# Spreading the rows of a routing list over steps of attention and products of TensorE

## The chip, the cores and the metric

The kernel runs on one core of one Trainium2 chip. The metric is the device time of one execution in microseconds; several executions are made and their median is given. Beside them one execution is taken with the hardware profiler, which records every instruction of the core's engines and every DMA packet.

## The reference: linear attention, then a mixture of experts with sticky routing

Attention has 8 batches, 8 heads, 576 positions and 64 features a head. Queries and keys are projected to 128 features, less the largest magnitude of the row, and both signs are exponentiated, so 256 features come out. For each head `kv` is the sum over positions of features times values, `z` the sum of features, and the output is `q_phi @ kv / (q_phi @ z + 1e-6)`. The heads are laid side by side: 4608 tokens of 512 features.

Each token then goes to one of 8 experts. It takes the expert with the largest gate logit, or, where a second gate's sigmoid is at least 0.5, the expert of the token before it (within its batch). The expert is `relu(x @ w1[e]) @ w2[e]` with 1024 hidden features, and its output is scaled by the softmax weight of that expert's logit.

```python
e = fresh_e if s == 0 or local_gate[b, s] < 0.5 else prev_e
out[b, s] = p[e] * (np.maximum(x[b, s] @ w1[e], 0.0) @ w2[e])
```

## The kernel before, in words

**Attention.** Method `step` runs once for each pair of 128-position chunks, 72 steps in all, and writes TensorE's order out by hand: a projection (line 351), turning queries (371), sums of keys and values (403), and numerators (483) of earlier pairs. The logits of two batches are complete after every 18 steps and go to `gate(bp)`, bp 0 to 3.

**Gates.** `gate` is a generator: each `yield STEP` ends its share of one step, and `chores` (from `step`) advances each generator in the list `background` once a step. It finds each token's expert and its rank in the expert's list (four small TensorE products, lines 738, 750, 767, 780 to 785, each needing a small PSUM space of which there is one a step, `turn_comes`). At its end it writes the list: nine indirect DMAs from GpSimd's queue (line 836), each scattering 128 rows (token number, weight, 64 bytes a row) into the DRAM tensor `lst`. One transfer is issued a step. `paced` puts each behind a copy on GpSimd (`tick`, line 646) that waits for that step's maxima.

**Early plan.** `plan_early`, a fourth generator, waits until gate 1's rows are written (`while self.scattering`), holds two more steps, gathers six pieces of the list (line 902), waits three steps, turns them on TensorE (line 933), and gathers the tokens' rows (line 1223) one a step. They feed two early slots e0 and e1 of three times 128 tokens each. Meanwhile the weights of e0 are split into high and low parts (lines 575 and 577), half a tile a step.

**Tail.** After the last step `tail` is set. Gate 2's generator in `background` has rows left: after `drained` it issues at most five (`ROW`) at once and holds the others until gate 3's ranks are out. Gate 3 (`last_gate`) is advanced by hooks inside slot e0's first layer: `soon[0]` is a list of functions, and `layer1` calls one at each of its 16 pauses (two for each block f of hidden features). The eleventh, `rest`, runs gate 3 to its end, and gate 2's held rows between. All these rows go to GpSimd's queue one behind the other, with no other wait than gate 3's ranks.

**Main plan.** In e0's second layer `later[0]` begins with `listed`, which advances `plan_main` twice: the plan itself (a chain of small VectorE operations from line 996 on, after the product of line 942), then `fetch`: row numbers, the list gathers `lr<-lst` (line 902, each made to wait for every row scattered), and between them `duals`, the plan of half-filled pieces (lines 1066 to 1091). Then follow the three transposes (line 1252) of e1's tokens. `layer2` calls the next function behind the blocks f = 0 and f = 2 of each piece of 128 tokens. In e1's first layer `read`, at the tenth pause, turns the gathered list on TensorE (line 933), and the main slots' rows are gathered after it.

**Order of the rest.** From the tail on a scheduler orders each engine's instructions by when they are ready in its own forecast, within the edges that `issue_after` and `behind_it` set (the second is a semaphore wait). An engine runs its queue in that order.

Of the kernel before, what the change touches and what calls it, by code (L numbers as in the profile page):

```python
# [39 lines left out]
QUOTA = 16  # L40
LINE = 256

STEP = "step"

# [35 lines left out]
class Kernel:  # L82
# [9 lines left out]
    def run(self):  # L92
        nc, tc, A = self.nc, self.tc, self.A
        act, dve = self.act, self.dve
        with ExitStack() as root:
# [38 lines left out]
            n = NBP * NHP * NC  # L134
# [36 lines left out]
            plan = self.plan_main()  # L171
            go = self.advance

            def rest():
                for _ in self.last_gate:
                    if self.ranked is not None:
                        for x in self.background:
                            for _ in x:
                                pass

            def listed():
                next(plan)
                next(plan)

            def read():
# [2 lines left out]
            no = lambda: None  # L188
            m = []
# [13 lines left out]
            def singles():  # L203
                more()
                m[0]()
            self.slots(self.eslots, soon=[[no, no, no, go, no, no, go, no, no, go, rest],
                                          [no] * 9 + [read, a[0], a[1], no, a[2], no, a[3]]],
                       later=[[listed], [no, no, singles] + [lambda k=k: m[k]() for k in (1, 2, 3)] + [more]])
            back.close()
            self.mid.close()  # L210
            self.open_rest(root)
# [487 lines left out]
    def gate(self, bp):  # L699
# [123 lines left out]
        tc.keep_in_program_order(dve.tensor_copy(pr[:, :, 0], self.tokid[:, bp * NC:bp * NC + NC]))  # L823
        dve.tensor_mul(pr[:, :, 1], se, su)
        self.scattering = True
        for c in range(NC):
            yield STEP
            while self.tail and not self.drained:
                yield STEP
            if self.tail and self.ranked is None:  # L830
                self.late += 1
                while self.late > ROW and self.ranked is None:
                    self.held_back = True
                    yield STEP
            with self.paced():
                ins = pool.indirect_dma_start(self.lst[:, :], bass.IndirectOffsetOnAxis(ri[:, c:c + 1], 0),
                                              pr[:, c, :], None)
            if self.late > ROW:
                self.behind_it(ins, self.ranked, "it would hold the last gate's chain")
            tc.declare_no_dep(ins.ins, group="scatter", reason="scattered rows are distinct")  # L840
            tc.add_to_no_dep_group("scatter", ins.ins)
            self.scattered.append(ins)
# [543 lines left out]
    def layer2(self, s, between, held=None):  # L1386
        tc, dve, pool = self.tc, self.dve, self.pool
        hh, hl = s["h"]
        self.need(s, 8) if len(s["ei"]) == 1 else None
        for k in range(s["n"]):  # L1390
            if hasattr(self, "psr"):
                t = self.psr.tile([128, DM], F32, name="l2")
            else:
                t = self.psb.tile([128, DM], F32, name="l2", tag="nm")
            m = min(128, s.get("cols", s["n"] * 128) - k * 128)
            o = slice(k * 128, k * 128 + m)
            for f in range(8):
                c = slice((f % 2) * DM, (f % 2) * DM + DM)
                self.both(s, 4 + f // 2, t[0:m], hh[:, f, o], hl[:, f, o], c, f == 0, f == 7)
                if f in ((0, 2) if s["n"] > 1 else (1, 3, 5)) and between:  # L1400
                    between.pop(0)()
                if f % 2 and k == s["n"] - 1:
                    self.used(1)
                elif f % 2:
                    self.spare()
            last = held is not None and k == s["n"] - 1
            y = self.mx2.tile([128, DM], F32, name="yl", bufs=1) if last else self.mx2.tile([128, DM], F32, name="y")
            u = s["u"] + k
            if last:
                w = s["prob"][0:m, u:u + 1]  # L1410
                self.act.activation(y[0:m], t[0:m], AF.Copy, scale=w)
            elif hasattr(self, "psr"):
                self.marks[dve] = dve.tensor_scalar_mul(y[0:m], t[0:m], s["prob"][0:m, u:u + 1])  # L1413
            else:
                self.marks[self.act] = self.act.activation(y[0:m], t[0:m], AF.Copy, scale=s["prob"][0:m, u:u + 1])
                self.last_y = self.marks[self.act]

            def put(y=y[0:m], at=s["tok"][0:m, u:u + 1]):
                ins = pool.indirect_dma_start(self.A["out"], bass.IndirectOffsetOnAxis(at, 0), y, None,  # L1419
                                              bounds_check=NT - 1, oob_is_err=False)  # L1420
                tc.declare_no_dep(ins.ins, group="outs", reason="each token is written once")
                tc.add_to_no_dep_group("outs", ins.ins)
            if last:
                held.append(put)
            else:
                put()

    def slots(self, order, held=None, soon=(), later=()):
# [19 lines left out]
        for i, s in enumerate(order):  # L1448
# [16 lines left out]
            else:  # L1465
                self.layer1_two(s, [])
            if i < len(later):
                rest = list(later[i]) + rest
            self.layer2(s, rest, None if new else held)
            for f in rest:  # L1470
                f()
# [132 lines left out]
```

## Time and profile before

| | us |
|---|---|
| median of 3 runs | 715.51 |
| lowest, highest | 713.83, 719.53 |
| the profiled execution, its own time | 712.14 |
| its span, first to last instruction | 710.3 |
| TensorE busy, weight loads busy | 698.4, 617.9 |
| VectorE, ScalarE, GpSimd busy | 460.7, 411.8, 265.0 |

The profiled execution lies 3.37 us under the median; 1.84 us of its time lie outside the span. The views are a page of totals; tables of waits; tables of busy time by stretch; and the instructions in order of time. An instruction row gives its start and duration, the engine, the line, what it writes and reads, the shapes and the count; in brackets stands the idle time before it and what ended it.

### The profile page before, as it was taken

To read this page: it belongs to the slowest core of one execution; us is meant where nothing else is said; L and a number is where in the kernel's file an instruction comes from. 1 tells how busy PE (TensorE), PEld (TensorE's weight loads), DVE (VectorE), ACT (ScalarE), POOL (GpSimd) and SP (SyncE) were. 2 spreads that over 40 slices of the span, in tenths; PEclk is the share of its full clock that TensorE was granted. 3 is DMA by queue.
4 is the path that set the end of the run, shared out by engine and by line. 5 is a ranking of instruction groups with operands and counts; after the bars stand their busy time and mean duration, and the time that the engine had idled before them with its cause. 6 is when DMAs were issued, how large, how long until landed. Compare 5 with 4: busy or idle time off the path is not lost. (4 is left out here: it accounts for less than half of the span.)

```text
span 710.3 us, 22974 instructions
## 1 busy us (share of the span) xinstructions
PE 698.4 (98%) x9576; PEld 617.9 (87%) x9576; DVE 460.7 (65%) x876; ACT 411.8 (58%) x888; POOL 265.0 (37%) x532
## 2 busy tenths in 40 slices
PE   7999999999999999999999999999999999999996
PEld 6999999999999999888887986889888877888985
DVE  6898899889998995683537446535643367554522
ACT  5777776777768873434465654745754269471512
POOL 0211101430146675562345551345744236443311
PEclk9999999999999999999999999999999999999998
DMA  7855545555466863254818975344886375444200
GB/s 232 268 154 148 160 124 155 148 149 161 134 183 198 252 189 113 64 181 129 280 70 294 405 279 194 135 149 150 265 307 252 110 243 172 150 163 155 76 27 31
DMA packets 66074, 125.17 MB, mean 176 GB/s; under 512 B 7180, under 2 KB 45260, under 8 KB 65910
## 3 DMA queue, kind: packets, MB, share of 16 engines
q1 hardware_dynamic: 57680, 100.90, 44.8%
q0 software_dynamic: 7968, 22.58, 9.0%
q8 instruction: 76, 1.25, 0.7%
q14 instruction: 30, 0.25, 0.1%
q10 hardware_dynamic: 320, 0.20, 0.1%
HBM read 102.11 MB, written 21.80 MB: 174 GB/s over the span
## 5 line engine op out<-in xcount | busy, mean ns | idle before, releaser
L1173 DVE TENSOR_TENSOR wlo<-wraw,whi 128x1024 fp32r<-128x1024 f32 x80 | 96.4, 1222 | 37.8 <-ACT whi L1170 37.5
L1305 PE MATMUL l<-whi,hh 128*128 128x512 f32 (+1 forms) x288 | 113.4, 394 | 0.5 <-ACT hh L1358 0.5
L1306 PE MATMUL l<-wlo,hh 128*128 128x512 f32 (+1 forms) x288 | 112.7, 391 | 0.8 <-DVE wlo L1173 0.8
L1307 PE MATMUL l<-whi,hl 128*128 128x512 f32 (+1 forms) x288 | 112.6, 391 | 0.0
L362 ACT ACTIVATE kp<-sb 128x512 f32<-128x512 f32 x144 | 83.3, 623 | 48.9 <-DVE sb L359 48.1
L1359 DVE SCALAR_TENSOR_TENSOR hl<-l,hh 128x512 fp32r<-128x512 f32 (+3 forms) x84 | 50.4, 600 | 93.2 <-ACT hh L1358 93.1
L1170 ACT CAST whi<-wraw 128x1024 fp32r<-128x1024 f32 x80 | 82.4, 1047 | 43.8 <-PE l L1307 27.0
L1358 ACT ACTIVATE hh<-l 128x512 fp32r<-128x512 f32 (+3 forms) x84 | 44.0, 525 | 108.9 <-PE l L1307 57.2
L1305 PE MATMUL l<-xhi,whi 128*128 128x384 f32 (+4 forms) x308 | 106.8, 347 | 0.0
L1307 PE MATMUL l<-xhi,wlo 128*128 128x384 f32 (+4 forms) x308 | 106.5, 346 | 0.0
L1306 PE MATMUL l<-xlo,whi 128*128 128x384 f32 (+4 forms) x308 | 106.4, 345 | 0.0
L358 DVE TENSOR_REDUCE m<-pj 128x8 f32<-128x1024 f32 (+1 forms) x74 | 88.3, 1193 | 20.4 <-PE pj L351 18.3
L1285 POOL COPY xg<-z 32x128 f32<-32x128 f32 x208 | 70.4, 339 | 58.7 <-DVE z L1273 41.4
L359 DVE TENSOR_TENSOR sb<-pj,m 128x1024 f32<-128x1024 f32 (+1 forms) x74 | 88.5, 1196 | 5.6
L351 PE MATMUL pj<-first,kq 64*128 64x128 f32 x1152 | 85.3, 289 | 3.5 <-DMA first<-in_first 3.4
L483 PE MATMUL nm<-kvs,qp 128*64 128x73 f32 x2304 | 86.3, 227 | 0.5 <-issue 0.4
L1419 POOL DMA_INDIRECT out<-y,p_tokm x31 | 37.4, 1205 | 127.2 <-DVE y L1413 126.0
L386 ACT ACTIVATE qp<-pj 128x512 f32<-128x512 f32 x144 | 78.1, 596 | 8.4 <-PE pj L371 7.5
L483 PEld LDWEIGHTS nm<-kvs,qp 128*64 128x64 f32 x2304 | 79.1, 137 | 1.0 <-issue 0.7
L351 PEld LDWEIGHTS pj<-first,kq 64*128 64x128 f32 x1152 | 71.4, 190 | 9.4 <-DMA first<-in_first 3.4
L403 PE MATMUL kvp<-v,kp 128*64 128x65 f32 x2048 | 75.3, 224 | 0.1
L1285 ACT COPY xg<-z 32x128 f32<-32x128 f32 x208 | 61.7, 296 | 20.3 <-DVE z L1273 16.0
(266 smaller groups left out, 1080.0 us busy)
## 6 DMA issues: line engine op xcount, KB each, us to landing
wraw<-in_w1h SPq DMA_DIRECT2D x44, 512.0 KB, 5.1
wraw<-in_w2h SPq DMA_DIRECT2D x44, 512.0 KB, 5.6
kq<-in_kqT SPq DMA_DIRECT2D x47, 384.0 KB, 4.1
v<-in_va SPq DMA_DIRECT2D x48, 195.0 KB, 3.5
xs<-xo SPq DMA_DIRECT2D x48, 128.0 KB, 2.4
whi<-in_w1h SPq DMA_DIRECT2D x8, 512.0 KB, 5.8
wlo<-in_w1h SPq DMA_DIRECT2D x8, 512.0 KB, 8.6
whi<-in_w2h SPq DMA_DIRECT2D x8, 512.0 KB, 7.2
```

What stands on the lines that cost most here:

```text
L351: self.last_pe = self.pe.matmul((q if j else t)[:, h, i % 2, j, :], kq[r, j, s], self.w2[r], start=True, stop=True)
L358: dve.tensor_reduce(m[:, a:a + n], x[:, s], AX.X, ALU.max, apply_absolute_value=True)
L359: self.last_dve = dve.tensor_sub(to[:, s], x[:, s], m[:, a:a + n].unsqueeze(2).broadcast_to([128, n, 128]))
L362: self.last_act = act.activation(kp[:, :, :, sg, :].rearrange("p c h f -> p h c f"), sb[:, :, :, 0], AF.Exp, scale=1.0 - 2 * sg)
L386: self.act.activation(qp[:, sg].rearrange("p h (c r k) -> p (h c) r k", c=2, r=2), src, AF.Exp, scale=1.0 - 2 * sg)
L483: self.last_num = self.pe.matmul(e["t"][r, c - c0, k], self.ch[i]["qp"][:, sg, h, q0 + r.start:q0 + r.stop], kvs[:, sg, k], start=sg == 0, ...
L1170: self.act.copy(hi, raw)
L1173: (low or self.dve).tensor_sub(lo[:, c], raw[:, c], hi.bitcast(F32)[:, c])
L1285: self.marks[engine] = copy(to[q, :, g], z[g, :, b, :])
L1305: mm(o, ah, bh, start=first, stop=False)
L1306: mm(o, ah, bl, start=False, stop=False)
L1307: self.last_pe = mm(o, al, bh, start=False, stop=last)
```

## The change

1. In the first gates (before the tail) a step ends only ahead of each even row, so that two transfers are issued a step, each behind its own `tick`.
2. Once gate 3's ranks are out, each row's transfer also waits for the last TensorE product written before it (`last_pe`).
3. `rest` is gone. Gate 3 gives a mark `LIST` when its rows are ready to be written. A generator `lists` runs to that mark, then through what `background` still holds and gate 3's rows. `row` advances it by one: at the last six pauses of e0's first layer, and at five places of its second.
4. In slot e0's second layer there are four places a piece instead of two (f = 0, 2, 4, 6). `later[0]` is now a whole order: `plan_row` (the plan's first part and a row), a token transpose, two rows, two transposes, two rows, `listed` (what rows are left, then the plan's second part with the list gathers). The transposes keep their places (f = 2 of the first piece, f = 0 and 2 of the second); the plan's second part moves from f = 0 of the first piece to f = 0 of the third.

```diff
--- before.py
+++ after.py
@@ -40,7 +40,7 @@
 QUOTA = 16
 LINE = 256
 
-STEP = "step"
+STEP, LIST = "step", "list"
 
 
 
@@ -171,15 +171,25 @@
             plan = self.plan_main()
             go = self.advance
 
-            def rest():
-                for _ in self.last_gate:
-                    if self.ranked is not None:
-                        for x in self.background:
-                            for _ in x:
-                                pass
+            def lists():
+                for x in self.last_gate:
+                    if x is LIST:
+                        break
+                for x in self.background + [self.last_gate]:
+                    for _ in x:
+                        yield
+            flow = lists()
+
+            def row():
+                next(flow, None)
+
+            def plan_row():
+                next(plan)
+                row()
 
             def listed():
-                next(plan)
+                for _ in flow:
+                    pass
                 next(plan)
 
             def read():
@@ -203,9 +213,9 @@
             def singles():
                 more()
                 m[0]()
-            self.slots(self.eslots, soon=[[no, no, no, go, no, no, go, no, no, go, rest],
+            self.slots(self.eslots, soon=[[no, no, no, go, no, no, go, no, no, go] + [row] * 6,
                                           [no] * 9 + [read, a[0], a[1], no, a[2], no, a[3]]],
-                       later=[[listed], [no, no, singles] + [lambda k=k: m[k]() for k in (1, 2, 3)] + [more]])
+                       later=[[plan_row, 0, row, row, 1, 2, row, row, listed], [no, no, singles] + [lambda k=k: m[k]() for k in (1, 2, 3)] + [more]])
             back.close()
             self.mid.close()
             self.open_rest(root)
@@ -823,8 +833,11 @@
         tc.keep_in_program_order(dve.tensor_copy(pr[:, :, 0], self.tokid[:, bp * NC:bp * NC + NC]))
         dve.tensor_mul(pr[:, :, 1], se, su)
         self.scattering = True
+        if self.tail:
+            yield LIST
         for c in range(NC):
-            yield STEP
+            if self.tail or c % 2 == 0:
+                yield STEP
             while self.tail and not self.drained:
                 yield STEP
             if self.tail and self.ranked is None:
@@ -837,6 +850,8 @@
                                               pr[:, c, :], None)
             if self.late > ROW:
                 self.behind_it(ins, self.ranked, "it would hold the last gate's chain")
+            if self.ranked is not None:
+                self.behind_it(ins, self.last_pe, "the list's rows are written one transfer after the other")
             tc.declare_no_dep(ins.ins, group="scatter", reason="scattered rows are distinct")
             tc.add_to_no_dep_group("scatter", ins.ins)
             self.scattered.append(ins)
@@ -1397,7 +1412,7 @@
             for f in range(8):
                 c = slice((f % 2) * DM, (f % 2) * DM + DM)
                 self.both(s, 4 + f // 2, t[0:m], hh[:, f, o], hl[:, f, o], c, f == 0, f == 7)
-                if f in ((0, 2) if s["n"] > 1 else (1, 3, 5)) and between:
+                if f in ((1, 3, 5) if s["n"] == 1 else (0, 2, 4, 6) if s is self.eslots[0] else (0, 2)) and between:
                     between.pop(0)()
                 if f % 2 and k == s["n"] - 1:
                     self.used(1)
@@ -1465,7 +1480,7 @@
             else:
                 self.layer1_two(s, [])
             if i < len(later):
-                rest = list(later[i]) + rest
+                rest = [x if callable(x) else rest[x] for x in later[i]]
             self.layer2(s, rest, None if new else held)
             for f in rest:
                 f()
```

## Rows read from the trace of the kernel before

**Rows 1.** The page's totals: span, TensorE, its weight loads, the granted clock by slices.
```profile
span 710.3 us, 22974 instructions
PE 698.4 (98%) x9576; PEld 617.9 (87%) x9576; DVE 460.7 (65%) x876; ACT 411.8 (58%) x888; POOL 265.0 (37%) x532
PEclk9999999999999999999999999999999999999998
```
**Rows 2.** What TensorE waited for: us in total, times, longest.
```profile
PE pj L351 <- DMA first<-in_first: 3.4, 1, 3.4
PE l L1306 <- DVE wlo L1173: 0.8, 1, 0.8
PE l L1305 <- ACT hh L1358: 0.5, 1, 0.5
PE nm L483 <- issue: 0.4, 1, 0.4
PE pj L371 <- issue: 0.3, 1, 0.3
```
**Rows 3.** One stretch: length; PE, PEld, DVE, ACT, POOL busy; clock, DMA share, GB/s.
```profile
193.00:226.00 33.00, 33.00 (x888) 31.54 (x886) 29.64 (x64) 24.85 (x57) 18.76 (x41) 1.00 0.69 199
```
**Rows 4.** TensorE in order of time, second layer of slot e0.
```profile
293.84 0.39 PE L1305 MATMUL l<-whi,hh 128*128 128x512 f32 x1
294.07 0.40 PE L1306 MATMUL l<-wlo,hh 128*128 128x512 f32 x1
```
**Rows 5.** GpSimd in order of time, first and later gates' rows and what follows them.
```profile
193.10 0.18 POOL L646 COPY tick<-m 128x1 f32<-128x1 f32 x1 [0.60 <-DVE m L358]
193.44 1.01 POOL L836 DMA_INDIRECT lst<-pr,ri  x1 [0.15 <-issue]
...
223.32 1.00 POOL L836 DMA_INDIRECT lst<-pr,ri  x1
...
231.00 0.92 POOL L902 DMA_INDIRECT lr<-lst,p_rie  x1 [0.55 <-issue]
...
265.38 1.03 POOL L836 DMA_INDIRECT lst<-pr,ri  x1 [0.16 <-issue]
...
289.61 0.96 POOL L836 DMA_INDIRECT lst<-pr,ri  x1 [5.42 <-DVE pr L78]
...
304.19 0.96 POOL L836 DMA_INDIRECT lst<-pr,ri  x1 [0.31 <-DMA lst<-pr,ri]
305.45 3.55 POOL L1419 DMA_INDIRECT out<-y,p_toke  x1 [0.30 <-issue]
```
**Rows 6.** TensorE in order of time, last steps of attention: the two waits put down to "issue".
```profile
256.91 1.23 PE L483 MATMUL nm<-kvs,qp 128*64 128x73 f32 x31 [0.40 <-issue]
...
266.59 0.40 PE L371 MATMUL pj<-first,sb 64*128 64x64 f32 x5 [0.29 <-issue]
```
**Rows 7.** Line 933 on TensorE (180 to 352): the early list is turned.
```profile
L933 PE MATMUL pj<-first,lr x2: 247/258/269, 239.7 to 239.8; 6*128 6x6 f32 x2
```
**Rows 8.** VectorE in order of time: the main plan.
```profile
298.35 0.15 DVE L1066 TENSOR_TENSOR p_hf<-p_um,p_um 54x8 f32<-54x8 int32 x1
...
303.74 0.13 DVE L1081 TENSOR_SCALAR p_rih<-p_kh 54x1 int32<-54x1 f32 x1
...
314.90 0.14 DVE L78 TENSOR_SCALAR p_rim<-p_rowm 54x1 int32<-54x1 f32 x1
```
**Rows 9.** GpSimd in order of time: the last list gather; then the landing of all of them.
```profile
316.32 0.92 POOL L902 DMA_INDIRECT lr<-lst,p_rim  x1 [0.31 <-issue]
...
DMA to landing us min/median/max: 4.0/5.0/5.3
```
**Rows 10.** TensorE in order of time, first layer of e1: the list is turned.
```profile
322.52 0.41 PE L933 MATMUL pt<-first,lr 34*128 34x34 f32 x2
```
**Rows 11.** ScalarE in order of time: the third output piece of e0.
```profile
314.04 0.69 ACT L1415 ACTIVATE y<-l,p_probe 128x512 f32<-128x512 f32 x1 [3.69 <-DMA out<-y,p_toke]
```
**Rows 12.** TensorE, first main slot, second layer: a wait for split weights.
```profile
375.28 0.19 PEld L1306 LDWEIGHTS l<-wlo,hh 128*128 128x128 f32 x1 [1.07 <-DVE wlo L1173]
```

## The prediction, made before the changed kernel ran

> **What bounds the kernel now.** I read the page's totals first. TensorE is busy 698.4 of 710.3 us, no other engine over 461, and its clock is granted at the upper level (2.4 GHz) in every slice but the last [rows 1]. So TensorE sets the end, and the change is worth what it does to TensorE's gaps. Next comes the table of what TensorE waited for [rows 2]: 3.4 us for the first load, and 0.8, 0.5, 0.4 and 0.3 us later, 2.0 together. The longest of those is at a main slot's second layer, where its weight load waits 1.07 us for split weights [rows 12]. Nothing in that table names the lists: no TensorE instruction waits for a row's transfer, a list gather or the plan. The reader is to see that the scattering, the change's subject, lies beside the bound. Of the idle 11.9 us (710.3 less 698.4), 5.4 are a first wait and these four; the rest is the last piece's way out and small gaps, which this change doesn't touch.
>
> Do hidden gaps leave more? Products of 512 columns start 0.23 us apart (293.84, 294.07) [rows 4], against 0.21 for 512 columns at 2.4 GHz, so the stream runs with at most some 0.02 us lost a product. The Trainium skill, "Perfetto Trace Analysis", section Identifying the Most-Contended Engine, says that matmul busy time does not tell the distance to roofline and that the share of weight loads does. By that rule 710.3 less 617.9, or 92 us, might be room; the spacing of the rows says that it is not, since a load is short beside 512 columns, and here the rows decide.
>
> **The change part by part.**
>
> *Two transfers a step in gates 0 and 1.* Nothing is added in number: 9 transfers and 9 ticks a gate. They take 5 steps instead of 9. A second tick and transfer in a step cost GpSimd 0.18 + 0.15 (the idle time between) + 1.01, or 1.34 us [rows 5]. In the stretch with gate 1's rows GpSimd is busy 18.8 of 33 us, or 57% [rows 3]; of a step of 3.7 us (eight steps from 193.44 to 223.32 [rows 5]) about 2.1 are used, and 1.6 left. The second transfer fits. Waiting behind it are the additions to the logits and the weight split, whose users come steps later. Cost 0; if that cover went, one step's 1.34 us less the 1.6 would still not show.
>
> *What follows earlier.* Gate 1's last row goes at 223.32 and the early list gather at 231.00 [rows 5]. Four steps fewer, at 3.7 us, put the gather near 216 and its turning (239.7 [rows 7]) near 225. The six gathers of tokens and their ticks move forward as much, out of the last steps of attention. The weights of e0 go half a tile a step either way. Also, the early list's turning takes the one PSUM space of its step, in which gate 2 would have had its second product; with it gone gate 2 comes one step earlier. So where before one row of gate 2 went out ahead of the tail (265.38 [rows 5]), four do now (two steps of two), and the five that the tail allows finish it. No row of gate 2 is left for e0's first layer.
>
> What is that worth? The two waits that the trace puts down to "issue", 0.4 and 0.3 us [rows 2], both lie in the last steps of attention, at 256.91 and 266.59 [rows 6], where these gathers, gate 2's operations and the weight split meet. From below: 0, if they come from the splits, which stay. From above: both, 0.7, and as much again for what is late beside them without idling the engine, 1.4 in all. They could also just move, or grow where gate 2 now lies: +0.7 by the same rows. I take a gain of 0.3, nearer to 0 since nothing shows what ends those waits.
>
> *Gate 3's rows, each bound to a product.* Before, 12 transfers run from 289.61 to 304.19 + 0.96 [rows 5], or 1.3 us each. After, nine. The first `row` carries gate 3 to its mark, at the pause where `rest` was; five follow at the next five pauses, about 1 us apart (a block of 12 products of 384 columns, 1.92 us at 2.4 GHz, has two pauses). GpSimd takes 1.3 us a transfer and stays the slower, so these five end near 297. The other four go with the second layer: at f = 0, 4 and 6 of the first piece and f = 4 of the second, the last near 303.5, by counting 0.69 us a block of three products from 293.84 [rows 4] and 0.21 for the four transposes of 128 columns that each token piece takes. That is where the last one went before (304.19). TensorE gets no instruction and no wait, so this is 0 on it. Behind each waiting row on GpSimd stand only output pieces and list gathers. The first output piece waited for the queue until 305.45 and took 3.55 us; ScalarE then waited 3.69 us for that buffer, at 314.04 [rows 5, 11], and TensorE didn't wait even so. Now that piece goes near 301. Gain on the path 0, from below 0, from above 0.3 (the lowest ScalarE entry in rows 2, halved for one place).
>
> *The plan's second part, moved by two pieces.* The first part keeps its place. The moved instructions are two for row numbers, some 29 of `duals`, and three gathers. Their users are e1's turning of the list at 322.52 [rows 10] and the main gathers behind it. Before, the last list gather goes at 316.32 [rows 9], 1.3 us after its row number (314.90 [rows 8]); with the median landing of 5.0 us it is there at 321.3, 1.2 ahead of TensorE. After, f = 0 of the third piece is near 306 by the same count, long before 314.9. The question is whether `duals` then stands behind the first part on VectorE. Before, its operation of line 1066 ran at 298.35, 16 us ahead of row numbers that are written before it in the code [rows 8], so the scheduler fills in by readiness, and VectorE's total is the same. Then the last gather is as early as it was: 0. If they are put strictly behind, 29 operations at 0.08 (filled) to 0.2 us (one waiting for the other) make 2.3 to 5.8 us, less some 2 by which the first part is relieved; the last gather is then up to 3.8 us later and TensorE waits up to 3.8 - 1.2, or 2.6 us. I take 0.
>
> For the margin: the Trainium skill, "DMA: Bandwidth & Descriptors", section Anatomy of one DMA (SWDGE path), gives 2.0 us and bytes over 436e3 a transfer. A gather of 34 list pieces of 8 KB would then take 2.6 us, an estimate by that page, and TensorE would have 3.6 us to spare instead of 1.2, so that even the strict order would cost almost nothing. The rows have 4.0 to 5.3 us [rows 9], and I go by them.
>
> **The sum.** Profiled execution 712.14 - 0.3 + 0 + 0 = 711.8. The median of the runs shown lies 3.37 above that execution, so the time to predict is 715.2.
>
> **The rivals.**
>
> *A: the end of attention gets cleaner and the main slots with it.* The gathers move away, both issue waits go with what they delay (1.4), and the changed order of VectorE and ScalarE in the tail removes the wait of 1.07 us for split weights [rows 12]: 2.5 us, 712.7 as a median. For it: the waits lie just there. Against: the split weights' wait is 60 us behind the change.
>
> *B, the other side: the list arrives late.* The plan's second part stands behind its first on VectorE, the last gather lands after 322.5, and TensorE waits in e1's first layer, and again where the main slots' rows come as much later. It decides from 1.2 us of delay of the last gather. One wait of 2.6 us gives 717.8. For it: a margin of 1.2 us is thin, and the code now names the gathers two pieces, some 11 us, later. Against: the scheduler's filling in [rows 8].
>
> *C: the rows queue up.* A row bound to a product holds up GpSimd's queue, output pieces hold their buffers longer, and weights and list gathers come late in several slots. At 1.07 us a slot as in rows 12, seven slots make 7.5 us: 722.7. Against: GpSimd is given fewer rows there than before, and no product that is waited for is later than the old queue's end.
>
> *D: it doesn't do what it says.* The rows of the tail were already 1.3 us apart, so GpSimd keeps them in the same places, and nothing changes: 715.5. This can't be told from the forecast by time.
>
> **How the numbers follow.** Chances: forecast with D 0.64, A 0.18, B 0.14, C 0.04. One per cent of this kernel, 7.2 us, is about what a measurement can tell from no change; of the cases only C passes it. The idle time that could be won at all past the first load is 2.0 us by rows 2, so faster by over 1% has no mechanism here; 0.03 is left for what I don't see. Slower by over 1%: C and something for mechanisms not thought of, 0.05. Within 1%: 0.92. The range runs from A's 712.7, less 1 for the spread of the runs (713.83 is 1.7 under the median), to B's 717.8 and as much above: 711.7 to 718.8.
>
> **What would show it right or wrong.** Right: pairs of transfers 1.3 us apart in steps of gates 0 to 2; the early list gather near 216 and its turning near 225; four rows of gate 2 ahead of the tail and five in it; nine rows after 289, the last near 304; the turning of the main list between two products with no wait in front; TensorE's busy time the same within 1 us. Wrong: a wait of TensorE for line 933, for `tr` or for `hh` between 278 and 345 (B), a list gather that starts after 318, or TensorE waits for split weights in several main slots (C).

## The result, and the profile after

The changed kernel takes 722.78 us (median of 12 runs, 719.40 to 724.14); the kernel before, run beside it 12 times, takes 717.37 us (713.83 to 721.14). The ratio is 1.0069, with a 95% interval of 1.0052 to 1.0086: slower by 0.7%, where 715.2 us and no measurable difference were forecast. The time lies above the range that was given. (All ratios here are taken over all executions and can differ from the quotient of the two medians by up to 0.25%; an unchanged kernel, before_again below, came out at 1.0019.)

A caution for all that follows: the profile of before was taken in an execution of 712.14 us, 5.2 under the median of 717.37. So the two profiles lie 10.3 us apart where the medians lie 5.4 apart. The steps below explain the profiles; what makes up the difference is taken up under "Closeness, number or rows".

The page's totals of the changed kernel, to be laid beside [rows 1]:
```profile
span 720.7 us, 22984 instructions
PE 703.4 (98%) x9576; PEld 620.3 (86%) x9576; DVE 461.5 (64%) x876; ACT 411.7 (57%) x888; POOL 266.0 (37%) x535
PEclk9999999999999999999999999999999999999999
```
The span is 10.4 us longer. The clock is granted at the same level (2.4 GHz) throughout, and TensorE has the same 9576 products. Its idle time grows from 11.9 to 17.3 us, and its busy time by 5.0: a group of products that is held up in its middle counts partly as busy.

What TensorE waited for, in the order of [rows 2]:
```profile
PE pj L361 <- DMA first<-in_first: 3.4, 1, 3.4
PE kvp L413 <- issue: 2.9, 7, 1.2
PE nm L493 <- issue: 1.0, 1, 1.0
PE pj L381 <- issue: 0.9, 2, 0.4
PE pj L381 <- DVE sb L369: 0.8, 2, 0.5
PE l L1321 <- DVE wlo L1188: 0.8, 1, 0.8
PE pj L469 <- issue: 0.5, 1, 0.5
```
Nearly all that is new stands at lines of attention, and most of it is put down to "issue", to nothing that the profile shows; before, there were 0.4 and 0.3 us of this kind. The wait for split weights [rows 12] is unchanged. So the time isn't lost in the tail, where the forecast looked for trouble, but in attention.

Where in attention? Set the starts of the projections (line 351 before, 361 after) side by side, step by step. Until 128 us the two profiles stay within 0.3 us of each other. Then four steps lose 0.69, 0.77, 0.80 and 0.79 us, and later five lose 1.14, 0.82, 1.02, 0.88 and 0.26: 7.2 us. Eight of these nine are the steps in which gates 0 and 1 write two rows; the last one, with 0.26, follows them and writes one. Two steps at 242 to 252 us lose 1.51 and 1.00. All else to the last step comes to zero within 0.2, and 0.7 is lost behind it.

The first of those steps, all engines in order of time:
```profile
127.88 1.07 POOL L849 DMA_INDIRECT lst<-pr,ri  x1 [0.69 <-issue]
...
128.32 1.16 PE L361 MATMUL pj<-first,kq 64*128 64x128 f32 x16
...
128.95 0.20 POOL L656 COPY tick<-m 128x1 f32<-128x1 f32 x1
...
129.32 1.02 POOL L849 DMA_INDIRECT lst<-pr,ri  x1 [0.17 <-issue]
...
129.78 0.48 PE L413 MATMUL kvp<-v,kp 128*64 128x65 f32 x7
...
130.67 0.76 PE L413 MATMUL kvp<-v,kp 128*64 128x65 f32 x18 [0.41 <-issue]
...
130.79 1.23 DVE L368 TENSOR_REDUCE m<-pj 128x8 f32<-128x1024 f32 x1 [1.69 <-PE pj L381]
130.92 0.60 ACT L396 ACTIVATE qp<-pj 128x512 f32<-128x512 f32 x1 [1.41 <-PE pj L381]
```
The second transfer goes out 1.44 us behind the first, as soon as GpSimd is free. The projection has ended at 129.48, and VectorE's maxima should follow at once. They start at 130.79, 0.45 us after the second transfer's issue ends (129.32 + 1.02 = 130.34). ScalarE's exponentials come at 130.92, and TensorE's sums stop in the middle of a group until 130.67. Three engines stop together and go on together behind the second transfer's issue. In the kernels with one transfer a step (tail_again, before_again) TensorE has no such stop.

The other loss, TensorE at 242 to 252 us, with the six gathers of tokens and the loads that they now meet:
```profile
243.81 0.80 PE L413 MATMUL kvp<-v,kp 128*64 128x65 f32 x19
245.86 0.62 PE L413 MATMUL kvp<-v,kp 128*64 128x65 f32 x13 [1.25 <-issue]
...
251.74 0.73 PE L493 MATMUL nm<-kvs,qp 128*64 128x73 f32 x16 [0.96 <-issue]
```
The busy time by stretch (columns as in [rows 3]; the last two are the DMA engines' share and GB/s), of the changed kernel:
```profile
242.00:246.00 4.00, 2.75 (x60) 2.34 (x56) 3.83 (x9) 3.19 (x8) 2.87 (x7) 1.00 0.95 298
246.00:250.00 4.00, 4.00 (x109) 3.82 (x109) 3.19 (x8) 2.47 (x7) 2.37 (x6) 1.00 0.92 299
```
The DMA engines are nearly full here. That alone is not the loss: unbound, a later run with the gathers in the same place, has them as full and TensorE busy throughout:
```profile
242.00:246.00 4.00, 4.00 (x108) 3.85 (x106) 3.87 (x11) 3.22 (x10) 2.72 (x5) 1.00 0.96 325
```
The traces show what TensorE waits for: its own next instructions. Among the DMA queues is one that carries instructions:
```profile
q8 instruction: 76, 1.25, 0.7%
```
These are 76 packets of 16 KB for the 19324 instructions of TensorE in the trace, its weight loads among them: one packet for about 256 instructions, every 4.8 us in attention. Here one comes 7.6 us behind the one before it (243.67 after 236.09) and ends at 244.63, and TensorE goes on 1.23 us later; the stop at 251.74 ends 1.47 us behind the end of the next. In the traces of all runs, 21 of TensorE's stops in attention that are put down to "issue" and last over 0.15 us end 1.2 to 1.5 us behind the end of such a packet, and all 21 at instruction number 193 or 194 of a block of 256. The two waits of the kernel before, at 256.91 and 266.59 [rows 6], are among them (1.24 and 1.48 us). All the other stops of this kind end within 1.7 us of the start of a row's transfer, at other instruction numbers, so those are something else. That the packet is late because the DMA engines are full is likely, but no run tried it alone.

What was forecast of the order did come. GpSimd in order of time:
```profile
223.51 0.92 POOL L917 DMA_INDIRECT lr<-lst,p_rie  x1 [0.39 <-issue]
...
271.23 1.04 POOL L849 DMA_INDIRECT lst<-pr,ri  x1 [0.16 <-issue]
272.63 0.99 POOL L849 DMA_INDIRECT lst<-pr,ri  x1 [0.16 <-issue]
...
275.82 1.00 POOL L849 DMA_INDIRECT lst<-pr,ri  x1
277.18 0.99 POOL L849 DMA_INDIRECT lst<-pr,ri  x1 [0.16 <-issue]
```
The early list gather is at 223.51 instead of 231.00 (about 216 without the time lost ahead of it), and four rows of gate 2 go out ahead of the tail.

### The profile page after: what moved, and what is told of

The parts are those of the page before. It is cut to its first block, busy times and chain, and to the rows that moved or that the text cites. A ratio compares the mean times of both kernels' runs of the same rounds, so it can differ in the third digit from the quotient of the medians.

```text
span 720.7 us, 22984 instructions
## 1 busy us (share of the span) xinstructions
PE 703.4 (98%) x9576; PEld 620.3 (86%) x9576; DVE 461.5 (64%) x876; ACT 411.7 (57%) x888; POOL 266.0 (37%) x535
## 5 line engine op out<-in xcount | busy, mean ns | idle before, releaser
L1434 POOL DMA_INDIRECT out<-y,p_tokm x31 | 39.0, 1259 | 126.2 <-DVE y L1428 125.0
L413 PE MATMUL kvp<-v,kp 128*64 128x65 f32 x2048 | 78.3, 225 | 3.2 <-issue 2.9
L413 PEld LDWEIGHTS kvp<-v,kp 128*64 128x64 f32 x2048 | 67.4, 137 | 7.7 <-issue 4.2
```

Source lines behind the costliest of these rows:

```text
L413: self.pe.matmul(t[r, sg, h], kp[:, h, sg, r], v[:, h], start=first and sg + h == 0, stop=last and sg + h == 2)
```

## The experiments

Eighteen experiments ran, some of them repeats, in five groups. A group ran on one chip, with the kernel before beside it; the five groups had five different chips.

| kernel | kernel before there, us | this, us | ratio (95% interval) |
|---|---|---|---|
| tail_only | 713.38 | 712.13 | 0.9983 (0.9964 to 1.0002) |
| pairs_only | 713.38 | 714.18 | 1.0008 (0.9986 to 1.0029) |
| twin | 713.38 | 714.34 | 1.0004 (0.9985 to 1.0023) |
| busy | 713.38 | 715.64 | 1.0038 (1.0015 to 1.0062) |
| again | 716.68 | 722.24 | 1.0071 (1.0046 to 1.0095) |
| unbound | 716.68 | 722.51 | 1.0077 (1.0045 to 1.0108) |
| late_plan | 716.68 | 720.58 | 1.0051 (1.0034 to 1.0068) |
| early_plan | 716.68 | 719.94 | 1.0043 (1.0019 to 1.0067) |
| again2 | 715.96 | 722.69 | 1.0101 (1.0079 to 1.0122) |
| pairs_again | 715.96 | 723.69 | 1.0108 (1.0089 to 1.0126) |
| tail_again | 715.96 | 713.23 | 0.9956 (0.9936 to 0.9977) |
| spaced | 715.96 | 723.53 | 1.0099 (1.0079 to 1.0119) |
| before_again | 716.38 | 716.36 | 1.0019 (0.9996 to 1.0043) |
| padded | 716.38 | 716.87 | 0.9994 (0.9968 to 1.0019) |
| twin_again | 716.38 | 732.31 | 1.0227 (1.0192 to 1.0261) |
| twin16 | 716.38 | 732.64 | 1.0252 (1.0213 to 1.0291) |
| mended | 713.46 | 712.59 | 0.9981 (0.9965 to 0.9996) |
| tail_third | 713.46 | 712.82 | 1.0002 (0.9988 to 1.0015) |

### The parts alone

**tail_only**: the changed kernel with one transfer a step in attention.
```diff
-            if self.tail or c % 2 == 0:
-                yield STEP
+            yield STEP
```


> The changed kernel with one transfer a step again in the first gates; the tail's bound rows and its new order stay. Theory 1 (a second indirect transfer right behind the first one on GpSimd holds up the other engines): the loss is in attention alone, so the steps 34 to 38 and 52 to 56 have their old lengths and the time is that of the kernel before, 715 to 718.5 us. Theory 2 (the rows bound to products, or the later list gathers, cost): the loss stays, 721 to 724 us.

**pairs_only**: the kernel before with two transfers a step and nothing else.
```diff
-            yield STEP
+            if self.tail or c % 2 == 0:
+                yield STEP
```


> The kernel before with nothing but the two transfers a step in the first gates. Theory 1: the whole loss of the changed kernel is here, 721 to 724 us, and each step with a pair is 0.7 to 1.1 us longer in the profile. Theory 2: 715 to 718.5 us.

**twin**: the kernel before; each row in attention is followed by a second transfer of the same 128 rows, into a tensor that nothing reads.
```diff
+            if not self.tail:
+                with self.paced():
+                    twin = pool.indirect_dma_start(self.lst2[:, :], bass.IndirectOffsetOnAxis(ri[:, c:c + 1], 0),
+                                                   pr[:, c, :], None)
```


> The kernel before, one row a step as it was, but each row of the first gates (19 before the tail) is followed by its own tick and a second scatter of the same 128 rows into a DRAM tensor that nothing reads. No part of the computation is changed; the early plan keeps its time. Theory 1: 19 pairs of 0.7 to 1.1 us in the profile, 13 to 21 us, and 7 to 20 us in the plain runs. Theory 3 (the loss comes from the plan that moves four steps earlier, and from what it then meets): no loss, 715 to 719 us.

**busy**: as twin, with an addition on GpSimd (0.78 us) in place of the second transfer.
```diff
+                with self.paced():
+                    pool.tensor_add(self.busy, self.busy, self.busy)
```


> The kernel before, one row a step, but each row of the first gates is followed by a tick and an addition on GpSimd of about 1 us on a tile of its own, in place of a second transfer. Theory 1: no loss, 715 to 719 us, since there is no second transfer. Theory 4 (GpSimd is busy too long in a step, and what stands behind it is late): the loss of twin, 13 to 21 us in the profile.

Measured, on one chip: tail_only is clean, and so, against all expectation, are pairs_only and twin. The step with the first pair in pairs_only, where the instructions stand as in the changed kernel:
```profile
127.87 1.07 POOL L837 DMA_INDIRECT lst<-pr,ri  x1 [0.69 <-issue]
...
129.31 1.02 POOL L837 DMA_INDIRECT lst<-pr,ri  x1 [0.17 <-issue]
...
129.52 1.23 DVE L358 TENSOR_REDUCE m<-pj 128x8 f32<-128x1024 f32 x1 [0.42 <-PE pj L351]
...
129.78 1.15 PE L403 MATMUL kvp<-v,kp 128*64 128x65 f32 x32
129.88 1.08 ACT L386 ACTIVATE qp<-pj 128x512 f32<-128x512 f32 x2 [0.37 <-PE pj L351]
```
The transfers lie at the same places within 0.02 us, and nothing stops: the maxima start 1.27 us sooner than in the changed kernel. The other loss was there: the steps that start at 234.8 and 239.6 us lose 0.98 and 1.82 us. Busy lost 0.2 to 0.85 us in four steps of gate 1, none in gate 0: GpSimd's time there isn't free either, but that is another loss, on a chip where the pairs cost nothing.

So the changed kernel's loss belonged either to the program (the second half of the change) or to the chip; the two were not yet told apart.

### The other suspects

**again** is the changed kernel once more. **unbound** takes away the binding of gate 3's rows to products, **late_plan** keeps the early plan where it was.
```diff
-            if self.ranked is not None:
-                self.behind_it(ins, self.last_pe, "the list's rows are written one transfer after the other")
...
-        for _ in range(0 if self.tail else HOLD):
+        for _ in range(0 if self.tail else HOLD + 4):
```
**early_plan** is the kernel before with the early plan three steps sooner and no pairs (`WAIT, HOLD = 2, 0` for `3, 2`).

> The changed kernel itself, once more, beside the runs of before that the other experiments have, since neither half of the change alone showed a loss outside its interval. Theory 5 (the two halves lose only together, or the loss is the chip's): 0.7% slower than before again if it is the two together, within 0.2% if it belonged to the first chip. The profile tells whether the eight steps with pairs are 0.7 to 1.1 us longer again.

> The changed kernel without the wait of each row for a product (the rows stay in their new places of the program). Theory 2 (the bound rows cost): the loss goes, 0.7% under the changed kernel. Theories 1 and 3: the time of the changed kernel within 0.2%.

> The changed kernel with the early plan held four steps longer, so that its token gathers go where they went in the kernel before, while the rows still go two a step. Theory 3 (the gathers of tokens, moved four steps forward, meet the last loads of keys, queries and values): the two long steps 64 and 65 (2.6 us together in the changed kernel's profile) have their old lengths, and the time is 2 to 3 us under the changed kernel's. Theory 1: no difference to the changed kernel.

> The kernel before with its early plan three steps earlier (two steps less held, one less waited), one row a step, nothing of the change. Theory 3: steps around 63 to 66 lose 1 to 3 us, 0.2 to 0.4% slower than before. Theory 1: as before, within 0.1%.

Measured: again repeats the result, with the same losses in the steps with two transfers. The other loss it doesn't repeat: its two steps near 242 us lose 0.42 and 0.18 us in place of 1.51 and 1.00, and those of unbound, again2 and pairs_again lose nothing. Unbound is as slow as again (722.51 and 722.24): the binding is not the cost. Late_plan takes 1.7 us less than again (2 to 3 were expected), and its two steps near 242 us lose nothing:
```profile
242.00:246.00 4.00, 4.00 (x109) 3.73 (x106) 3.79 (x10) 3.46 (x10) 2.13 (x6) 1.00 0.57 168
```
With the token gathers later, the DMA engines are used to 0.57 (0.95 in the changed kernel's first profile, 0.86 in again's), and TensorE is busy all four microseconds. So the moved gathers cost something, but how much varies from one profile to the next: 2.5 us in these steps in the first, 0.6 in again's, nothing in unbound's. That fits a stop that comes only where a packet of instructions falls due while the DMA engines are full. The losses of the pairs stay. Early_plan is slower for a reason of its own, in TensorE's waits:
```profile
PE pj L933 <- DMA lr<-lst,p_rie: 4.1, 1, 4.1
```
One step of waiting was taken from the list, and the list is late; of the gathers it tells little.

### Chip or program

Four kernels on one chip, two of them old ones. **again2** is the changed kernel, **pairs_again** is pairs_only, **tail_again** is tail_only, to the letter. **spaced** is the changed kernel with the second transfer of a step paced behind the step's exponentials.
```diff
-        return self.tc.issue_after(self.pool.tensor_copy(t, self.m[:, 0:1]).ins)
+        return self.tc.issue_after(self.pool.tensor_copy(t, self.kp_new[:, 0, 0, 1, 127:128] if apart else self.m[:, 0:1]).ins)
```


> The changed kernel once more, on the same chip as the other three of this call. So far every run that lost 0.7 to 1.1 us in each of the eight steps with two transfers was on a chip where the kernel before takes 716.7 to 717.4 us, and the runs without that loss (pairs_only, twin) were on one where it takes 713.4. Theory C1 (the loss belongs to the chip: some chips hold up the engines behind the second transfer, others don't): here this kernel and pairs_again show the same in these steps, both with the loss or both without it; without it this kernel is at most 1.003 of the kernel before. Theory C2 (the loss belongs to the program: the second half of the change brings it about): this kernel loses 7 us in these steps on any chip (ratio 1.006 to 1.009), pairs_again none.

> The kernel before with two transfers a step in gates 0 and 1 and nothing else. C1: in the eight steps it does what the changed kernel does in this call; with the loss it takes 1.006 to 1.010 of the kernel before (7 us, and 1 to 2.5 for the token gathers). C2: no loss in the eight steps, 0.999 to 1.003.

> The changed kernel with one transfer a step in attention. Both theories: no loss in the steps of attention, 0.996 to 1.001 of the kernel before, as in its first run.

> The changed kernel, but the second transfer of a step is paced behind that step's exponentials (the second half of kp) and not behind its maxima: the pair lies some 2.4 us apart instead of 1.4. Theory S1 (it is the second transfer right behind the first that holds up the engines): the losses of the eight steps go, 1.000 to 1.003. Theory S2 (any second transfer in a step costs it, since its place in the step is what matters): 0.7 to 1.1 us a step stay, 1.006 to 1.009. If again2 has no loss in these steps here, this run tells nothing of them.

Measured: pairs_only, 1.0008 on the first chip, is 1.0108 here, and loses what again2 loses, step by step, the fifth of each gate being the one behind its pairs (0.81, 0.80, 0.87, 0.85, 0.62 and 1.28, 0.96, 1.01, 0.90, 0.30 us; again2: 0.81, 0.82, 0.88, 0.85, 0.62 and 1.21, 0.97, 1.04, 0.95, 0.26). Its first pair now:
```profile
127.79 1.07 POOL L837 DMA_INDIRECT lst<-pr,ri  x1 [0.69 <-issue]
...
129.24 1.02 POOL L837 DMA_INDIRECT lst<-pr,ri  x1 [0.17 <-issue]
...
130.63 0.98 PE L403 MATMUL kvp<-v,kp 128*64 128x65 f32 x26 [0.41 <-issue]
...
130.76 1.22 DVE L358 TENSOR_REDUCE m<-pj 128x8 f32<-128x1024 f32 x1 [1.74 <-PE pj L371]
130.89 1.08 ACT L386 ACTIVATE qp<-pj 128x512 f32<-128x512 f32 x2 [1.45 <-PE pj L371]
```
The same program stops on this chip and not on the other. That the tail's half of the change brings it about falls; the pairs bring it about, on some chips. The busy time of 120 to 220 us says it in one line for a run, by the count of TensorE's products in 100 us (second x). pairs_only, then pairs_again:
```profile
120.00:220.00 100.00, 100.00 (x2658) 95.27 (x2655) 90.29 (x187) 71.68 (x167) 34.99 (x87) 1.00 0.56 158
```
```profile
120.00:220.00 100.00, 96.02 (x2439) 89.43 (x2437) 83.80 (x179) 65.01 (x152) 30.94 (x79) 1.00 0.50 144
```
219 products fewer at 26.6 a microsecond are 8.2 us. The kernel before has 2655 in its first profile, tail_again 2658.

Spaced failed as an experiment, and told something all the same. GpSimd's transfers and what stopped behind them:
```profile
132.05 1.04 POOL L849 DMA_INDIRECT lst<-pr,ri  x1 [0.16 <-issue]
...
133.45 0.98 POOL L849 DMA_INDIRECT lst<-pr,ri  x1 [0.16 <-issue]
...
134.08 0.41 PE L493 MATMUL nm<-kvs,qp 128*64 128x73 f32 x5 [0.43 <-issue]
134.17 1.15 ACT L372 ACTIVATE kp<-sb 128x512 f32<-128x512 f32 x2 [0.88 <-DVE sb L369]
```
The transfer at 132.05 is the second of its step, 2.1 us behind the first, and nothing stops at it. The one at 133.45 is the first of the next step, only 1.40 us behind, and there the engines stop. Closeness had only been handed to the next step, and the loss went with it.

### Closeness, number or rows

**before_again** profiles the kernel before. **padded** is pairs_only with an addition of 64 elements a partition (0.29 us) and its tick between the two transfers of a step. **twin_again** is twin; **twin16** writes 16 rows with the second transfer.
```diff
+            if not self.tail and c % 2:
+                with self.paced():
+                    pool.tensor_add(self.pad, self.pad, self.pad)
             with self.paced():
                 ins = pool.indirect_dma_start(self.lst[:, :], bass.IndirectOffsetOnAxis(ri[:, c:c + 1], 0),
...
-                    twin = pool.indirect_dma_start(self.lst2[:, :], bass.IndirectOffsetOnAxis(ri[:, c:c + 1], 0),
-                                                   pr[:, c, :], None)
+                    twin = pool.indirect_dma_start(self.lst2[:, :], bass.IndirectOffsetOnAxis(ri[0:16, c:c + 1], 0),
+                                                   pr[0:16, c, :], None)
```


> The kernel before, with a profile on the chip of this call. If its median is near 716 (a chip like those that lost), its attention steps should be as in the first profile within 1 us in all (one transfer a step costs nothing, as in tail_again), and the 3 us between the chips lie in the stretch where rows go out 1.3 us apart, 284 to 310 us, or behind it. If its median is near 713, the chip is like the one without the loss and the other three tell little.

> pairs_only with an addition of 64 elements a partition on GpSimd between the two transfers of a step, so that they start some 1.85 us apart instead of 1.44, and the next step's first about as much later. Theory K1 (closeness: a transfer issued 0.3 us behind another holds up the engines): losses of the eight steps go to under 0.2 us each, ratio 0.999 to 1.004. Theory K2 (two transfers in 3.7 us are too many, however spaced): 0.6 us or more a step stay, ratio 1.006 to 1.011.

> The kernel before, each row in attention followed by a second transfer of the same rows to a tensor that nothing reads, 19 times. K1 and K2, and any theory in which the transfer itself is the cause, not the list: 0.7 to 1 us lost in each such step, 13 to 19 us in all, ratio 1.015 to 1.026, on a chip that loses at all. If the list's own dependencies were the cause, as on the chip without the loss: 1.000 to 1.003.

> As twin_again, the second transfer with 16 rows instead of 128. If the rows written (descriptors and packets) make the cost: an eighth to a quarter of twin_again's loss, ratio 1.002 to 1.007. If the issue on GpSimd makes it, whatever the rows: as twin_again, 1.015 or more.

Measured on a chip where the kernel before takes 716.38 us: twin_again loses 15.9 us (nothing on the first chip), padded 0.5. Padded's first pair:
```profile
128.22 1.07 POOL L843 DMA_INDIRECT lst<-pr,ri  x1 [0.69 <-issue]
...
129.87 1.22 DVE L358 TENSOR_REDUCE m<-pj 128x8 f32<-128x1024 f32 x1 [0.43 <-PE pj L351]
...
130.03 1.04 POOL L843 DMA_INDIRECT lst<-pr,ri  x1 [0.17 <-issue]
130.12 1.15 PE L403 MATMUL kvp<-v,kp 128*64 128x65 f32 x32
...
131.90 1.00 POOL L843 DMA_INDIRECT lst<-pr,ri  x1 [0.15 <-issue]
```
As many transfers as in pairs_only, 1.81 and 1.87 us apart in place of 1.44, and the maxima and the sums go through. Pairs_only itself did not run on this chip; that it stops close transfers is shown by twin_again. GpSimd does more in these steps than in pairs_only, so its being busy is not the cause either. The steps still lose 0.35, 0.52, 0.30, 0.24 and 0.07 to 0.54 us: the stop is mostly gone, not wholly, so the expectation of under 0.2 us each was too clean. Over 120 to 220 us, padded, then twin16:
```profile
120.00:220.00 100.00, 99.58 (x2587) 94.06 (x2585) 88.08 (x184) 69.30 (x160) 36.15 (x101) 1.00 0.54 152
```
```profile
120.00:220.00 100.00, 94.86 (x2300) 87.38 (x2294) 79.51 (x172) 61.63 (x144) 37.81 (x91) 0.98 0.47 131
```
Twin16 loses as much as twin_again with an eighth of the rows in the second transfer (its issue still takes 0.90 us in place of 1.02): it is the issue, not the rows written.

Before_again answers where the 3 us between the chips lie. Its attention is as in the first profile within 1.1 us. Its stretch from 300 to 340 us, then that of tail_again:
```profile
300.00:340.00 40.00, 38.09 (x193) 33.17 (x192) 23.82 (x108) 13.30 (x21) 18.31 (x16) 1.00 0.48 148
```
```profile
300.00:340.00 40.00, 40.00 (x207) 35.57 (x206) 25.73 (x117) 16.42 (x24) 18.11 (x17) 1.00 0.55 170
```
In the kernel before, 12 rows go out 1.27 us apart ahead of and into this stretch, and TensorE falls 14 products and 1.9 us behind the kernel with the tail's half of the change. But it isn't the stop of the pairs: the longest wait there ends 15 us behind the last row's issue, and is for VectorE's `hl`:
```profile
321.42 0.44 PE L1305 MATMUL l<-xhi,whi 128*128 128x384 f32 x1 [1.13 <-DVE hl L1359]
```
Pairs_again, with the tail of before, is at 40.00 in this stretch. So what the chip costs the kernel before in the tail stays open. It is, however, what makes the medians differ by less than the profiles: on such a chip it loses 3.2 us behind attention against its first profile (before_again), and the tail's half of the change wins 2.7 of them back (tail_again). That half and the pairs pull against each other in the measured 5.4 us.

Closeness isn't the whole condition either. In the changed kernel's tail five rows go out 1.28 us apart, from 289.14 to 294.25, and TensorE has no gap and as many products (37) as the kernel before in the same work:
```profile
289.00:295.00 6.00, 6.00 (x37) 5.63 (x36) 4.10 (x18) 1.63 (x4) 4.64 (x5) 1.00 0.14 39
```
What of attention has to be there for the stop was not tried.

### Both causes taken away

**mended** is the changed kernel with padded's addition and late_plan's delay; **tail_third** is tail_only beside it.

> The changed kernel with the addition of padded between the two transfers of a step (1.85 us apart) and the early plan held back as in late_plan. If closeness and the moved gathers are all of the loss: the eight steps together lose under 3 us, steps 64 and 65 nothing, and the ratio to the kernel before is 0.995 to 1.001. If something else in the changed kernel costs: 1.003 or more.

> tail_only a third time. 0.994 to 0.999 of the kernel before where that takes 716 us or more, 0.997 to 1.000 where it takes 713; 0 to 3 us under mended.

Measured, on a chip where the kernel before takes 713.46 us: mended 0.9981, tail_third 1.0002; they are 0.2 us apart. Mended loses nothing at 242 us, and of its pair steps nothing; but this chip may be one of those on which pairs don't stop, so of closeness it says nothing. Of the versions, the change without its pairs (tail_only) was never measurably slower, and on the chip of again2 it beats the kernel before by 0.4% and the whole change by 1.3% (713.23 and 722.69).

## Why the prediction was wrong

*What bounds the kernel*: right. TensorE sets the end, and all that was lost was lost in its gaps and held-up groups.

*Two transfers a step in gates 0 and 1*: **this is the step that failed**. It reckoned the second transfer's 1.34 us against 1.6 us free on GpSimd, found that "the second transfer fits", and put the cost at 0, and at nothing even with the cover gone. It does fit: in pairs_only, with both transfers in each step, no step with a pair loses anything. But on other chips a transfer in attention that is issued 0.4 us behind the end of another one's issue holds up TensorE, VectorE and ScalarE, 0.7 to 1.1 us a step, 7.2 us in the profile. The argument asked only who waits behind the transfer in GpSimd's queue. The trace of before had no two transfers so close in attention, so it could not show this. A cost that no row shows should have been bounded from above: one transfer's 1.34 us in each of eight steps makes 10.7 us, and with that as its upper end the range would have held the result.

*What follows earlier*: the order came as forecast, the sign did not. A gain of 0.3 us was taken, 0.7 of loss as its bound; the six gathers, moved forward, meet the last loads, and 2.5 us go in the first profile (1.7 by late_plan's median against again's). The step looked at what the gathers leave, not at what they join. Nor were the two waits of 0.4 and 0.3 us the work of gathers, gate or splits on an engine: they are TensorE waiting for a packet of instructions, as said above.

*Gate 3's rows, each bound to a product*, and *the plan's second part*: 0 was taken for both. Unbound confirms the first. For the second, the last list gather goes at 326.50 and the list is turned at 333.5, 7.0 us later where it was 6.2, and TensorE doesn't wait. That the tail's half gains 2.7 us on one chip (tail_again) was not forecast. B, with its late list, did not come: TensorE has no wait for line 948, which turns the list (line 933 before).

*The sum and the signs.* Its base was low: the kernel before, 715.51 us in three executions, took 717.37 beside the changed kernel, which is 1.9 of the 7.6 us of the miss. A's 712.7 takes its 2.5 us off the forecast, which holds 0.3 of them already; off the kernel before it is 713.0. Of the signs, TensorE's busy time was to stay within 1 us and rose by 5.0; the signs of being wrong were all set in the tail. The one that came, a list gather after 318 (326.50), came only because all of the tail lies some 10 us later; TensorE has none of the waits named there.

C's time, 722.7, is what was measured, but its mechanism (rows that queue up in the tail and late weights in seven slots) is nowhere in the profile. The number fits by chance.

## What to carry to other kernels

Free time on the queue that issues transfers doesn't make a second transfer free: here, in attention and on some chips, 1.44 us from start to start stopped three other engines, 1.8 us nearly not, at the same number of transfers a step. Ask of each transfer that is moved forward which loads it will meet there, and count TensorE's own instructions, which come by DMA too, among those loads. And repeat a part alone on the chip that shows the effect before you clear it: pairs_only was innocent at 1.0008 and guilty at 1.0108, the same program.

## What was not expected of the hardware

The stop depends on the chip. On three of the five chips of the experiments the kernel before takes 716.0 to 716.7 us, and close transfers cost 0.6 to 1.3 us each in most steps; on the other two it takes 713.4 and 713.5, and where close transfers ran on one of these (pairs_only, twin) they cost nothing. The profiles differ in one more way: the first one of the kernel before and the six from the chips at 713 us (tail_only, pairs_only, twin, busy, mended, tail_third) have times from issue to landing for transfers; the 13 others, those without close transfers in attention among them, have none for any. Fewer semaphore events are recorded there too (8180 in tail_again, 9027 in tail_only), so "issue" says less in those profiles. What the chips differ in stays open, as does what the stop is; the engines go on together 0.3 to 0.6 us after the issue ends, and 16 rows stop them as long as 128.

The Trainium skill, "SBUF — State Buffer", section SBUF: two separate sides, states that on the engines' side of that memory only VectorE and GpSimd can hold each other up, at a shared port, and that TensorE and ScalarE never wait on anyone there. By that rule only VectorE could stop behind GpSimd; the rows above have TensorE's group interrupted and ScalarE late as well, so the rule doesn't account for this stop.
